# Turning keys and queries by VectorE in 32x32 blocks in a top-k attention and ELU feed-forward kernel

## The chip, the cores and the metric

The kernel runs on one core of a Trainium2 chip. The metric is the device time of one execution in microseconds. Three runs of the kernel before gave 1654.08, 1654.47 and 1656.92 us; the median is 1654.47 us.

A core has five engines with an instruction queue each, which is worked off in order: TensorE (PE, with a separate row PEld for weight loads), VectorE (DVE), ScalarE (ACT), GpSimd (POOL) and SyncE (SP), which here issues nearly all DMAs. Engines wait for each other through semaphores.

## The reference

```python
# q, k, v: (8, 8, 576, 64) float32; top_k = 32
scores = scale * np.matmul(q, k.transpose(0, 1, 3, 2))      # scale = 1/8
kth = np.partition(scores, -top_k, axis=-1)[..., -top_k:-top_k + 1]
scores = np.where(scores >= kth, scores, -1000000000.0)
scores = scores - np.max(scores, axis=-1, keepdims=True)
attn = np.exp(scores)
attn = attn / (np.sum(attn, axis=-1, keepdims=True) + 1e-09)
x = np.matmul(attn, v).transpose(0, 2, 1, 3).reshape(4608, 512)
h = x @ w_in                                                # (512, 2048)
g = np.where(h > 0.0, h, np.exp(np.minimum(h, 0.0)) - 1.0)
return g @ w_out                                            # (2048, 512)
```

The weights arrive as 64-bit floats and are converted to 32 bits on the chip.

## The kernel before

**Steps.** There are 8 batches of 8 heads. Heads go in pairs (`hp`, four a batch): partitions 0 to 63 hold the 64 dimensions of the first head of a pair, 64 to 127 those of the second. The 576 query rows of a batch are four tiles of 128 rows and one of 64. A step is one query tile with one head pair (for the tile of 64 rows, two pairs), 18 steps a batch and 144 in all. In even batches the tile of 64 rows comes last, in odd batches first.

**One step.** `scores` (L305) multiplies queries and keys on PE into two PSUM tiles, and ACT evicts them to `sc` with the scale (L313). VectorE then finds the 32nd largest value of each row: four times the eight largest (MAX8, lines 324, 334, 347, 359), with three passes in between that overwrite what was found (MATCH_REPLACE8, L328, L352). The first eight steps use `select_row`, where Tile's scheduler puts the instructions of each engine in order; later ones use `select`, in the order in which the program writes them (`manual_schedule` for PE, ACT, VectorE and POOL; SP's order is still the scheduler's). `mask` makes probabilities from the scores on ACT (L378, L381, L382) and POOL (L380), `normalise` divides them by their sums on POOL (L392 to L399), `turn` transposes them in 128x128 blocks on PE (L418, evicted by ACT at L419), `attend` multiplies them by v (L444), and `finish` puts the result into `xT` (L471).

**Feed-forward.** When the rows of a block are complete, its pieces join a list: `hidden` (L516 on PE; L526, L529, L531 on ACT), closing the ELU on VectorE (the gates, L488), and `project` (L541), with an output store (L550, L553). `feed` hands out pieces in every quarter of a step, by fixed costs and due times (L617 to L640); none of this depends on run time.

**In what order a step is written (from step 9 on).** Scores of the step two ahead, attention of a finished group, the first two passes of the top-k, pieces, mask of the step before, `turn_qk`, more passes, `turn` of the step two back, more passes and pieces, `normalise`, `turn_qk(True)`.

**Weights.** In the first ten steps `decode_piece` converts 32 pieces of the weights. A piece takes passes on POOL (L174, L191), three on ACT (L180, L181, L183) and one on VectorE (L187); eight raw buffers take the loads (L153).

**Keys and queries.** `load_qk` (L222) loads a head pair so that partition p holds the rows 4p to 4p+3 of both heads, 256 bytes for each row and head, and puts the last 64 rows of keys and queries into a fifth chunk of the key tile. Six DMAs go out for a pair. There are two buffers of each tile. `transpose_qk` (L255) is a generator: PE transposes the fifth chunk (L264), ACT copies it to two places (L267, L271); then for the keys, and after a `yield` for the queries, PE transposes four chunks (L275) and ACT copies them (L281). `turn_qk()` runs one part, `turn_qk(True)` the rest. So column c*128 + p of a head's queries is row 4p + c, and a query tile is every fourth row; `load_v` reads v in the same order (L247), and the output rows are written with a stride of four (L590). The first head's keys end in the last 64 rows, the second head's begin with them (L304), so that one chunk of the probabilities holds the rest of both heads.

`kqT` and `vT` have five buffers each. From batch 1 on, loads and turns are written at fixed steps before the first step `f` of the batch:

```python
plan = ((7, 5, 2), (5, 3, -2), (3, 1, -2), (1, -1, -3))
if b % 2 == 1:
    plan = ((7, 5, 0), (6, 4, -2), (5, 3, -3), (4, 2, -3))
for hp, (ahead, ready, late_v) in enumerate(plan):
    at(f - ahead, load_qk, b, hp)
    at(f - ready, start_qk, b, hp)
```

Of the kernel before, what the change touches and what calls it, by code (L numbers as in the profile page):

```python
# [10 lines left out]
FP32 = mybir.dt.float32  # L11
# [70 lines left out]
def kernel(  # L82
# [9 lines left out]
    nc = tc.nc  # L92
    P = nc.NUM_PARTITIONS
    B, H, S, D = q.shape
    dm, dff = moe_w_in.shape[0], moe_w_in.shape[1] // 2
    J = S // P
    JP = J * P
    R = S - JP
    HS = S // 2
# [2 lines left out]
    NF = dff // P  # L102
    NG = NF // 2
    T = 3 * P
    KEYS, QUERIES = R, R + S
    scale = 1.0 / float(D) ** 0.5
    assert D == 64 and R == 64 and J == 4 and H % 4 == 0 and dm == H * D == 512
    assert B % 2 == 0 and TOP_K % 8 == 0
# [1 line left out]
    def pool(name, bufs, **kw):  # L110
        return ctx.enter_context(tc.tile_pool(name=name, bufs=bufs, **kw))

    const = pool("const", 1)
    ldpool = pool("ld", 2)
    kvpool = pool("kv", 5)
# [7 lines left out]
    ps_t = pool("ps_t", 2, space=PSUM)  # L123
    ps_f = pool("ps_f", 2, space=PSUM)
    wide = [ps_sc.tile([P, 2, JP], FP32, tag=f"s{i}", name="scps") for i in range(2)]
# [6 lines left out]
    ident = const.tile([P, P], FP32, tag="ident", name="ident")  # L132
# [87 lines left out]
    loaded, kqT, vT = {}, {}, {}  # L220

    def load_qk(b, hp, other=nc.sync):  # L222

        for name, src in (("k", k), ("q", q)):
            n, queue = (J + 1, nc.sync) if name == "k" else (J, other)
            t = ldpool.tile([P, n, 2, D], FP32, tag=name + "in", name=name + "in")
            if name == "k":
                last = t
            for hh in range(2):
                queue.dma_start(  # L230
                    t[:, 0:J, hh, :],
                    src[b, 2 * hp + hh, 0:JP, :].rearrange("(p j) d -> p j d", j=J),
                )
            queue.dma_start(
                last[0:R, J, :, :] if name == "k" else last[R:P, J, :, :],
                src[b, 2 * hp : 2 * hp + 2, JP:S, :].rearrange("h p d -> p h d"),
            )
            loaded[b, hp, name] = t

    def load_v(b, hp):  # L240

        t = kvpool.tile([P, 2 * J + 2, D], FP32, tag="vT", name="vT")
        for hh in range(2):
            h = 2 * hp + hh
            nc.sync.dma_start(
                t[:, hh * J : (hh + 1) * J, :],
                v[b, h, 0:JP, :].rearrange("(p j) d -> p j d", j=J),  # L247
            )
            mine = slice(hh * R, (hh + 1) * R)
            other = slice((1 - hh) * R, (2 - hh) * R)  # L250
            nc.gpsimd.memset(t[other, 2 * J + hh, :], 0.0)
            nc.sync.dma_start(t[mine, 2 * J + hh, :], v[b, h, JP:S, :])
        vT[b, hp] = t

    def transpose_qk(b, hp):  # L255

        d = kvpool.tile([P, 4 * J + 3, D], FP32, tag="kqT", name="kqT")  # L260
        kqT[b, hp] = d[:].rearrange("p c d -> p (c d)")
        srcs = [loaded.pop((b, hp, name)) for name in ("k", "q")]
        ps = wide[0][:, 1, HS : HS + P]
        nc.tensor.transpose(  # L264
            ps, srcs[0][:, J, :, :].rearrange("p h d -> p (h d)"), ident[:]
        )
        nc.scalar.copy(  # L267
            d[:, 2 * J + 1 : 4 * J + 3 : 2 * J + 1, :],
            ps.rearrange("p (a s) -> p a s", a=2),
        )  # L270
        nc.scalar.copy(d[:, 0, :], ps[:, 0:R])  # L271
        for i, src in enumerate(srcs):
            ps = ps_t.tile([P, JP], FP32, tag="t", name="qkps")
            for c in range(J):
                nc.tensor.transpose(  # L275
                    ps[:, c * P : (c + 1) * P],
                    src[:, c, :, :].rearrange("p h d -> p (h d)"),
                    ident[:],
                )
            c0 = KEYS + i * (2 * J + 1) * D  # L280
            nc.scalar.copy(kqT[b, hp][:, c0 : c0 + JP], ps[:])  # L281
            yield

    def start_qk(b, hp):
        turning.append(transpose_qk(b, hp))
# [10 lines left out]
    def scores(u):  # L296

        u.sc = scpool.tile([P, 2, S], FP32, tag="sc", name="sc")
        q0 = QUERIES + u.t.qt * P
        for half in range(2):  # L300
            for h, i, rows in u.heads:
                kq = kqT[u.t.b, h // 2]
                part = slice(i * D, (i + 1) * D)
                k0 = (KEYS if i == 0 else 0) + half * HS  # L304
                nc.tensor.matmul(  # L305
                    wide[i][rows, half, 0:HS],
                    kq[part, q0 : q0 + u.t.ql],
                    kq[part, k0 : k0 + HS],
                    start=True,
                    stop=True,  # L310
                )
        for i in range(2):
            nc.scalar.activation(  # L313
                u.sc[:, i, :].rearrange("p (a s) -> p a s", a=2),
                wide[i][:, :, 0:HS], AF.Copy, scale=scale,
            )
# [253 lines left out]
    for b in range(B):  # L570
        if b % 2 == 0:
            rest = 2 * J
            division = [(0,), (1,), (2,), (3,), (rest,), (4, 5), (6, 7)]
            if b > 0:
                division = [(0, 1), (2, 3), (rest, 4, 5), (6, 7)]
            slots = {}
            for part in division:
                blk = Block(len(blocks), len(part))
                blocks.append(blk)
                slots.update((x, (blk, s)) for s, x in enumerate(part))  # L580
        first[b] = len(steps)
        tiles = []
        for qt in range(J + 1):
            r0 = b * S + (JP if qt == J else qt)
            if qt == J:
                (blk, slot), c0, n = slots[rest], (b % 2) * R, R
                rows = slice(r0, r0 + R)
            else:
                (blk, slot), c0, n = slots[(b % 2) * J + qt], 0, P
                rows = slice(r0, r0 + J * (P - 1) + 1, J)  # L590
            c0 += slot * P
            t = Tile(b, qt, rows, blk, slice(c0, c0 + n))
            blk.left += NHP
            blk.tiles[slot].append(t)
            tiles.append(t)
        order = [(0, 1), (2, 3), (J,)] if b % 2 == 0 else [(J,), (0, 1), (2, 3)]
        if b == 0:
            order[:2] = [(0,), (1,), (2,), (3,)]
        for qts in order:
            for hp in range(NHP // 2 if qts == (J,) else NHP):  # L600
                group = Group([tiles[qt] for qt in qts], hp)
                steps += [Step(tiles[qt], hp, group, i) for i, qt in enumerate(qts)]
            for qt in qts:
                n = len(steps)
                tiles[qt].block.ready = n + 1.0 if n <= tight else n + 2.5
# [11 lines left out]
    for b in range(1, B):  # L617
        f = first[b]
# [6 lines that stand above are left out]
            at(f - late_v, load_v, b, hp)  # L625
# [18 lines left out]
    E = mybir.EngineType  # L644
    engines = {E.PE, E.Activation, E.DVE, E.Pool}
    load_qk(0, 0, nc.scalar)
    load_weight(0)
    load_qk(0, 1)
    load_weight(1)
    load_v(0, 0)  # L650
    load_weight(2)
    with tc.manual_schedule(engines=engines):
        for hp in range(2):
            start_qk(0, hp)
            turn_qk(True)
            scores(steps[hp])
    load_qk(0, 2)
    load_qk(0, 3)
    for hp in range(1, NHP):
        load_v(0, hp)  # L660
# [8 lines left out]
    main, rest, other = slice(0, J), slice(J, J + 1), slice(J + 1, 2 * J + 1)  # L669
    for n in range(NS + 3):  # L670
# [3 lines left out]
        if n < tight:  # L674
            turn_qk(True)
            if n < 3:
                scores(ahead)
            if n > 1:
                scores(step(n + 3))
            for i in range(2):  # L680
                passes = select_row(cur, i, n < tight - 1)
                next(passes)
                if i == 0:
                    while closing:
                        attend(closing.pop(0))
                elif prev:
                    normalise(prev)
                    turn(prev, main)
                    turn(prev, rest)
                    turn(prev, other)  # L690
                feed(n, 0.25)
                next(passes)
                mask(cur, i, True)
                feed(n, 0.25)
            continue
# [64 lines left out]
```

## Time and profile before

| | |
|---|---|
| median of 3 runs | 1654.47 us |
| the profiled execution | span 1651.1 us from the first to the last instruction; the page gives no other time of it |
| mean granted TensorE clock | 0.976 |
| busy: PE, VectorE, ACT, POOL | 1592.8, 1496.6, 1152.7, 576.4 us |
| DMA queue q1 | 99792 packets, 54.26 MB, 11.8% of 16 engines |
| chain that ended last | PE 67%, VectorE 24%, ACT 4%, POOL 2% |

Busy time is the union of an engine's instructions. Instructions of an engine overlap at their ends: the time from one start to the next (the pitch) is shorter than the duration of one. A group's row gives line, engine, operation, tiles, shapes and count, then busy time and mean ns of one, then the idle time ahead and what ended it. A timeline row gives start and duration in us, then engine, line, operation and tiles; a count at the end means that several were merged.

### The profile page before, as it was taken

To read this page: it belongs to the slowest core of one execution; us is meant where nothing else is said; L and a number is where in the kernel's file an instruction comes from. 1 tells how busy PE (TensorE), PEld (TensorE's weight loads), DVE (VectorE), ACT (ScalarE), POOL (GpSimd) and SP (SyncE) were. 2 spreads that over 40 slices of the span, in tenths; PEclk is the share of its full clock that TensorE was granted. 3 is DMA by queue.
4 is the path that set the end of the run, shared out by engine and by line. 5 is a ranking of instruction groups with operands and counts; after the bars stand their busy time and mean duration, and the time that the engine had idled before them with its cause. 6 is when DMAs were issued, how large, how long until landed. Compare 5 with 4: busy or idle time off the path is not lost.

```text
span 1651.1 us, 25682 instructions
## 1 busy us (share of the span) xinstructions
PE 1592.8 (96%) x8528; PEld 1031.8 (62%) x8528; DVE 1496.6 (91%) x3044; ACT 1152.7 (70%) x2393; POOL 576.4 (35%) x1415
## 2 busy tenths in 40 slices
PE   5788999999999999999999999999999999999999
PEld 3476777666675757555566676656557575756564
DVE  6988999999999999999999999999989999998500
ACT  6898777678675867678576776768758585857521
POOL 4774333333333333333333333323323233332200
PEclk8579999999999999999999999999999999999999
DMA  7630110011100210011100210001200101000000
GB/s 227 188 116 8 44 38 20 7 29 44 35 1 14 52 43 8 7 29 44 29 13 1 56 30 28 1 21 36 50 13 1 36 8 29 7 7 7 7 13 13
DMA packets 101124, 56.19 MB, mean 34 GB/s; under 512 B 84096, under 2 KB 92288, under 8 KB 100992
## 3 DMA queue, kind: packets, MB, share of 16 engines
q1 hardware_dynamic: 99792, 54.26, 11.8%
q8 instruction: 68, 1.11, 0.3%
q14 instruction: 64, 0.52, 0.1%
q10 hardware_dynamic: 1200, 0.30, 0.1%
HBM read 45.09 MB, written 9.44 MB: 33 GB/s over the span
## 4 chain that ended last, share of the span: by engine, by line
PE 67%; DVE 24%; ACT 4%; POOL 2%; issue 1%; DMA 1%; SPq 0%; ACTq 0%; POOLq 0%; DVEq 0%
PE ops L541 24%; PE hps L516 22%; DVE wk L352 9%; DVE m L359 8%; PE avps L444 8%; PE scps L305 7%; PE eps L418 5%; DVE m L347 3%; DVE gT L488 1%; DVE wk L328 1%; PE qkps L275 1%; DVE m L334 1%; ACT sc L382 1%; PE scps L418 1%; ACT sc L381 1%
## 5 line engine op out<-in xcount | busy, mean ns | idle before, releaser
L359 DVE MAX8 m<-wk 128x8 f32<-128x576 f32 x816 | 574.7, 745 | 0.0
L516 PE MATMUL hps<-xT,w_in 128*128 128x256 f32 (+2 forms) x2432 | 546.1, 373 | 0.2 <-ACT xT L471 0.2
L541 PE MATMUL ops<-w_out,gT 128*128 128x512 f32 x1152 | 522.4, 598 | 0.0
L516 PEld LDWEIGHTS hps<-xT,w_in 128*128 128x128 f32 x2432 | 405.0, 192 | 97.5 <-issue 25.1
L352 DVE MATCH_REPLACE8 wk<-m,wk 128x576 f32<-128x576 f32 x544 | 399.3, 741 | 0.0
L541 PEld LDWEIGHTS ops<-w_out,gT 128*128 128x128 f32 x1152 | 208.5, 190 | 232.4 <-issue 219.5
L392 POOL TENSOR_SCALAR dene<-den 128x2 f32<-128x2 f32 x144 | 34.6, 240 | 818.9 <-ACT sc L382 818.5
L382 ACT ACTIVATE sc<-sc,den 128x576 f32<-128x576 f32 x288 | 223.5, 776 | 38.6 <-POOL den L380 14.5
L381 ACT ACTIVATE sc<-sc,m 128x576 f32<-128x576 f32 x288 | 227.0, 788 | 32.0 <-DVE m L359 31.9
L313 ACT ACTIVATE sc<-scps 128x576 f32<-128x576 f32 x288 | 173.3, 657 | 73.6 <-PE scps L305 73.4
L399 POOL TENSOR_SCALAR sc<-sc,rec 128x576 f32<-128x576 f32 x288 | 219.4, 772 | 15.0 <-POOL rec L397 0.2
L419 ACT COPY et<-eps 128x512 f32<-128x512 f32 x288 | 166.5, 578 | 80.1 <-PE eps L418 80.1
L305 PE MATMUL scps<-kqT 64*128 64x288 f32 (+1 forms) x1280 | 204.1, 443 | 18.3 <-ACT kqT L281 9.1
L444 PE MATMUL avps<-et,vT 128*64 128x256 f32 (+2 forms) x2080 | 194.7, 328 | 8.0 <-ACT et L419 7.5
L352 DVE MATCH_REPLACE8 wk<-m,sc 128x576 f32<-128x576 f32 x272 | 199.7, 741 | 0.0
L488 DVE SCALAR_TENSOR_TENSOR gT<-n,gT 128x512 f32<-128x512 f32 (+1 forms) x132 | 99.3, 752 | 107.6 <-ACT n L531 107.6
L418 PEld LDWEIGHTS eps<-ident,sc 128*128 128x128 f32 x1152 | 144.3, 144 | 82.0 <-issue 49.6
L347 DVE MAX8 m<-sc 128x8 f32<-128x576 f32 x272 | 191.1, 743 | 0.0
L418 PE MATMUL eps<-ident,sc 128*128 128x128 f32 x1152 | 176.5, 279 | 13.0 <-POOL sc L399 11.7
L444 PEld LDWEIGHTS avps<-et,vT 128*64 128x64 f32 x2080 | 123.1, 142 | 83.0 <-issue 25.1
L305 PEld LDWEIGHTS scps<-kqT 64*128 64x128 f32 (+1 forms) x1280 | 109.4, 183 | 89.0 <-issue 44.3
L526 ACT ACTIVATE n<-hps 128x512 f32<-128x512 f32 (+1 forms) x156 | 87.7, 562 | 83.1 <-PE hps L516 80.4
(49 smaller groups left out, 1089.1 us busy)
## 6 DMA issues: line engine op xcount, KB each, us to landing
kin<-in_k_dram SPq DMA_DIRECT2D x64, 128.0 KB, 2.9
raw<-in_moe_w_in_dram SPq DMA_DIRECT2D x16, 512.0 KB, 5.8
vT<-in_v_dram SPq DMA_DIRECT2D x64, 128.0 KB, 2.2
raw<-in_moe_w_out_dram SPq DMA_DIRECT2D x16, 512.0 KB, 3.4
out_dram<-osb SPq DMA_DIRECT2D x32, 256.0 KB, 2.3
qin<-in_q_dram SPq DMA_DIRECT2D x62, 128.0 KB, 2.8
kin<-in_k_dram SPq DMA_DIRECT2D x32, 32.0 KB, 2.5
vT<-in_v_dram SPq DMA_DIRECT2D x64, 16.0 KB, 2.1
```

The costliest lines, as they stand in the source:

```text
L305: nc.tensor.matmul(wide[i][rows, half, 0:HS], kq[part, q0 : q0 + u.t.ql], kq[part, k0 : k0 + HS], start=True, stop=True,)
L313: nc.scalar.activation(u.sc[:, i, :].rearrange("p (a s) -> p a s", a=2), wide[i][:, :, 0:HS], AF.Copy, scale=scale,)
L347: nc.vector.max(found[i], cur[i])
L352: nc.vector.match_replace(wk[i], found[i], cur[i], TAKEN)
L359: nc.vector.max(found[i], cur[i])
L381: nc.scalar.activation(sc, sc, AF.Prelu, scale=-1.0, bias=low, alpha=1.0 / STEEP)
L382: nc.scalar.activation(sc, sc, AF.Exp, scale=-STEEP, bias=gap, accum_out=u.den[:, i : i + 1])
L399: nc.gpsimd.tensor_scalar(u.sc[:, i, :], u.sc[:, i, :], rec[:, i : i + 1], 1.0, ALU.mult, ALU.mult)
L418: nc.tensor.transpose(ps[:, c * P : (c + 1) * P], sc[:, c0 : c0 + P], ident[:])
L444: nc.tensor.matmul(ps[i * D : (i + 1) * D, cols], vt[:, 2 * J + i if c == J else i * J + c, :], w, start=(c == 0), stop=(c == J),)
L516: nc.tensor.matmul(blk.h[:, f % bank, :], w_in[:, i, f * P : (f + 1) * P], blk.xT[:, i, 0:n_tok], start=(i == 0), stop=(i == NC - 1),)
L541: nc.tensor.matmul(blk.o[:], blk.gT[f // NG][:, f % NG, s * P : (s + 1) * P], w_out[:, f, :], start=(f == 0), stop=(f == NF - 1),)
```

## The change

Keys and queries are loaded as columns of half heads: partition 32*(2*hh + half) + i of the tile holds, for each of the 18 blocks n of 32 rows, the 32 dimensions of half `half` of row 32n + i of head `hh`. A piece is 32 floats, 128 bytes. One VectorE instruction for the keys of a pair and one for the queries then transposes every 32x32 block, which puts dimension d of head hh on partition 64*hh + d, with the rows in their natural order. The second head's last 64 keys are loaded into the first two blocks, so that the order of its keys is as before. A pair now takes ten DMAs, six for the keys and four for the queries. PE's nine transposes and ACT's four copies for a pair are gone. Since the rows are in natural order, v is read in rows of 256 bytes, and query tiles and output rows are contiguous. Loads and turns stay at the same places in the program.

```diff
-    KEYS, QUERIES = R, R + S
+    Q = 32
+    NB = S // Q
...
     def load_qk(b, hp, other=nc.sync):
-        for name, src in (("k", k), ("q", q)):
-            n, queue = (J + 1, nc.sync) if name == "k" else (J, other)
-            t = ldpool.tile([P, n, 2, D], FP32, tag=name + "in", name=name + "in")
-            if name == "k":
-                last = t
+        for name, src, queue in (("k", k, nc.sync), ("q", q, other)):
+            t = ldpool.tile([P, NB, Q], FP32, tag=name + "in", name=name + "in")
             for hh in range(2):
-                queue.dma_start(
-                    t[:, 0:J, hh, :],
-                    src[b, 2 * hp + hh, 0:JP, :].rearrange("(p j) d -> p j d", j=J),
-                )
-            queue.dma_start(
-                last[0:R, J, :, :] if name == "k" else last[R:P, J, :, :],
-                src[b, 2 * hp : 2 * hp + 2, JP:S, :].rearrange("h p d -> p h d"),
-            )
+                cut = NB if name == "q" or hh == 0 else NB - R // Q
+                for half in range(2):
+                    rows = slice((2 * hh + half) * Q, (2 * hh + half + 1) * Q)
+                    for lo, hi, to in ((0, cut, NB - cut), (cut, NB, 0)):
+                        if lo == hi:
+                            continue
+                        queue.dma_start(
+                            t[rows, to : to + hi - lo, :],
+                            src[
+                                b,
+                                2 * hp + hh,
+                                lo * Q : hi * Q,
+                                half * Q : (half + 1) * Q,
+                            ].rearrange("(n i) d -> i n d", i=Q),
+                        )
             loaded[b, hp, name] = t
...
     def load_v(b, hp):
-                v[b, h, 0:JP, :].rearrange("(p j) d -> p j d", j=J),
+                v[b, h, 0:JP, :].rearrange("(j p) d -> p j d", j=J),
...
     def transpose_qk(b, hp):
-        d = kvpool.tile([P, 4 * J + 3, D], FP32, tag="kqT", name="kqT")
-        kqT[b, hp] = d[:].rearrange("p c d -> p (c d)")
-        srcs = [loaded.pop((b, hp, name)) for name in ("k", "q")]
-        ps = wide[0][:, 1, HS : HS + P]
-        nc.tensor.transpose(
-            ps, srcs[0][:, J, :, :].rearrange("p h d -> p (h d)"), ident[:]
-        )
-        nc.scalar.copy(
-            d[:, 2 * J + 1 : 4 * J + 3 : 2 * J + 1, :],
-            ps.rearrange("p (a s) -> p a s", a=2),
-        )
-        nc.scalar.copy(d[:, 0, :], ps[:, 0:R])
-        for i, src in enumerate(srcs):
-            ps = ps_t.tile([P, JP], FP32, tag="t", name="qkps")
-            for c in range(J):
-                nc.tensor.transpose(
-                    ps[:, c * P : (c + 1) * P],
-                    src[:, c, :, :].rearrange("p h d -> p (h d)"),
-                    ident[:],
-                )
-            c0 = KEYS + i * (2 * J + 1) * D
-            nc.scalar.copy(kqT[b, hp][:, c0 : c0 + JP], ps[:])
+        d = kvpool.tile([P, 2, S], FP32, tag="kqT", name="kqT")
+        kqT[b, hp] = d
+        for i, name in enumerate(("k", "q")):
+            src = loaded.pop((b, hp, name))
+            nc.vector.transpose(d[:, i, :], src[:].rearrange("p n d -> p (n d)"))
             yield
...
     def scores(u):
-        q0 = QUERIES + u.t.qt * P
+        q0 = u.t.qt * P
-                k0 = (KEYS if i == 0 else 0) + half * HS
+                k0 = half * HS
-                    kq[part, q0 : q0 + u.t.ql],
-                    kq[part, k0 : k0 + HS],
+                    kq[part, 1, q0 : q0 + u.t.ql],
+                    kq[part, 0, k0 : k0 + HS],
...
-            r0 = b * S + (JP if qt == J else qt)
+            r0 = b * S + qt * P
-                rows = slice(r0, r0 + J * (P - 1) + 1, J)
+                rows = slice(r0, r0 + P)
```

## The prediction

> **What bounds the kernel now.** I read the page's first two parts first, for which engine is nearly full and when. The rows of part 2 are 40 slices of 41 us.
>
> ```profile
> PE 1592.8 (96%) x8528; PEld 1031.8 (62%) x8528; DVE 1496.6 (91%) x3044; ACT 1152.7 (70%) x2393; POOL 576.4 (35%) x1415
> ...
> PE   5788999999999999999999999999999999999999
> ...
> DVE  6988999999999999999999999999989999998500
> ```
>
> Both PE and DVE stand at 9 nearly throughout, so the averages decide nothing. The table by stretches does; its columns are us, then busy PE, PEld, DVE, ACT, POOL, granted clock, DMA share, GB/s.
>
> ```profile
> 0.00:164.00 164.00, 124.47 (x648) 89.14 (x649) 135.80 (x277) 134.82 (x275) 97.08 (x155) 0.78 0.44 135
> 164.00:700.00 536.00, 525.33 (x3234) 358.47 (x3234) 536.00 (x1100) 392.75 (x821) 190.11 (x502) 0.99 0.10 26
> 700.00:1552.00 852.00, 848.09 (x4325) 528.88 (x4322) 818.67 (x1661) 600.06 (x1250) 282.88 (x742) 1.00 0.08 22
> 1552.00:1651.00 99.00, 94.88 (x328) 55.27 (x326) 6.17 (x9) 25.04 (x49) 6.32 (x16) 1.00 0.04 14
> ```
>
> There are four stages. From 164 to 700 VectorE has no idle time at all: every added VectorE microsecond is paid. From 700 to 1552 PE is the fuller one (3.9 us idle) and VectorE idles 33.3 us. After 1552 the top-k is over and PE works off the feed-forward remainder. Before 164 neither is full, and I read the chain and the timeline there. The VectorE timeline puts the idle time of the third stage in front of the gates, as the list of waits does:
>
> ```profile
> DVE gT L488 <- ACT n L531: 107.6, 29, 44.5
> ```
>
> About 64 of the 107.6 us lie in the tail; 20.6 lie between 850 and 1341, and 12.8 after 1341.
>
> **The change, part by part.** *PE work removed.* Each of the 32 (batch, head pair) turns loses nine 128x128 transposes.
>
> ```profile
> 917.76 0.60 PE L275 MATMUL qkps<-ident,kin 128*128 128x128 f32 x4
> 918.19 0.60 PE L418 MATMUL eps<-ident,sc 128*128 128x128 f32 x4
> ```
>
> Four take 0.60 us but the next group starts 0.43 later, so the pitch is 0.11: 9 x 0.11 = 1.0 us a turn, 32 us in all, not the 50.7 us of the groups' summed durations (20.7 + 20.4 + 9.6). *ACT work removed:* two copies of 0.59, one of 0.25 and one of 0.21 a turn: 1.6 us, 53 in all. In the middle ACT is 70-73% busy, so this hides behind VectorE or PE; it counts only in the start.
>
> *VectorE work added.* 64 transposes of 128x576. No such operation is in the trace. The rows nearest in shape are these, with their pitch from the chain of waits:
>
> ```profile
> L359 DVE MAX8 m<-wk 128x8 f32<-128x576 f32 x816 | 574.7, 745 | 0.0
> ...
> 17.06 1.46 DVE wk L328 x2
> 18.52 1.32 DVE m L334 x2
> ```
>
> That is 0.66 us a MAX8 pass, 0.73 a match-replace pass. Lower end: the 128x512 shift of L187 mostly took 0.41, scaled 576/512 = 0.46. Upper end: two passes of 0.73 = 1.46, if a 4-byte block turn needs two. I take 0.67, the one-pass rows of the same width. The Trainium skill's page "VectorE: DVE Perf Modes", section "The three transpose paths", gives 311 ns for 128 columns of bf16 on VectorE and 390 ns on TensorE; scaled by 4.5 columns that would be an estimate of 1.40 us each and 47 us more in the sum. The trace's TensorE transposes come every 0.11 us, far below the page's figure, so I read that table as single latencies.
>
> *The steady part.* 56 transposes (batches 1 to 7) fall after 164. Those of batches 1 to 3 come before 700: 24 x 0.67 = +16 us, paid in full. The other 32 come before 1341 (the last batch turns at steps 121 to 124): +21.4, against the 20.6 us of VectorE waits on PE in that stretch. PE loses 16 us there and VectorE slows, so I expect most of that wait to go: -18. After 1341 nothing is turned, PE stays the limit, and only the lead that PE brings there counts: the eviction of a step's scores ends 20 to 25 us before the first top-k pass on them from 300 to 760, and 12 to 20 us before it later, so some 6 us of lead can come back; I take -4 (0 to -8). Together: 16 + 21.4 - 18 - 4 = +15. If no wait goes, +37; if every wait before 1341 goes and 8 in the tail, +9.
>
> *Waits that move.* The transposes sit in VectorE's queue in the midst of a step (keys) and at its end (queries). Queued behind them is the top-k itself, and who waits for that is ACT's mask. They wait for a load and for a free kqT buffer (five). In odd batches pair 1's buffer is freed by the scores issued at the start of the same step, 1.2 us of PE; PE leads or trails VectorE by about 3 us, so 0 to 3 us in four places, which I take as 0 since PE gains slack. Loads: in odd batches pairs 2 and 3 landed 14 to 19 us before use; four more DMA issues of 0.63 us take 2.5 of that. Other SP work (v, out) is queued behind, with longer margins. Cost 0; a missing load would stop the top-k for up to 10 us.
>
> *DMA volume.* 73,728 pieces of 256 B become 147,456 of 128 B, and v goes from 8,192 of 1 KB to 32,768 of 256 B. The packet records show 17.9 ns mean for 256 B and 9.0 for 4 B; between these, q and k need 83 to 165 us of each of 16 engines where they needed 82. The share in the middle is 0.08 to 0.10, and stays under 0.2: no cost. The page "DMA: Bandwidth & Descriptors" speaks against the change, in "Why small descriptors are slow (HBM only)": fixed cycles a packet, 11 for 256 B; the same formula makes 7 for 128 B, an estimate of 1.3 times the engine time, inside my bounds.
>
> *The start.* This is where order matters. Before, PE turns and ACT copies ran ahead, and the top-k of step 1 followed that of step 0 at once:
>
> ```profile
> 15.65 1.42 DVE L324 MAX8 m<-sc 128x8 f32<-128x576 f32 x2 [0.73 <-ACT sc L313]
> ...
> 20.85 1.19 ACT L313 ACTIVATE sc<-scps 128x576 f32<-128x576 f32 x2 [0.38 <-PE scps L305]
> ```
>
> Step 3 began at 45.6. In the changed kernel as built, VectorE's queue has pair 1's query transpose behind the last pass of step 0, pair 2's at the end of step 1, pair 3's at the end of step 2; each is directly ahead of the step whose scores need it. ACT's queue has the masks of step n ahead of the scores' eviction of step n+1, and PE's has the probability transposes of step 1 ahead of the scores of step 2. I follow it by hand. Keys land near 7, turned by 8.4; the first weight's conversion (loaded 1.2 us later) holds ACT until 12.0, so step 0 starts at 12.7 (3.0 earlier). A step is 9.63 us plus a key transpose: last pass at 23.0, query turned at 23.7. ACT masks until 25.8 (0.14 + 0.66 + 0.76 twice), converts a weight, evicts: step 1 at 28.9, 5.2 idle. Step 1 with a wait on a weight ends at 40.1, query at 40.8. Then masks (41.7), POOL's normalising (29.45 to 32.89 in the old timeline: 3.4), PE's eight transposes, scores, eviction: step 2 at 48.4, 7.6 idle. Step 2 ends at 58.7; masks and eviction give step 3 at 62.3, 2.9 idle. Against 45.6: +16.7.
>
> ACT tells the same from its side: until step 3 it idles 36 us of 62, where it idled 13 of 45.6. After that decode binds on ACT (gaps of 1 to 3 us only between 46 and 165), so 23 more idle minus 6 us of copies removed is +17. I take +16; bounds +3 (the later stalls before 164, 13.1 us on VectorE, all give way) and +27 (decode pieces that ran early now crowd steps 3 to 8: four more at 2 us, with three more waits).
>
> **Sum.** 1651.1 + 16 + 15 = 1682. The median run is 3.4 above the span of the profiled execution; with that, 1685.5.
>
> **Rivals.** (1) *PE decides to the end.* The chain that ended last is 67% PE. If the last 950 us are PE's alone and the start costs nothing, the gain is the removed PE pitch from 700 on, 16 us, plus 12 before it: 1654.5 - 28 = 1626 at best, 1638 with the later part only. Against it: VectorE's 536.00 of 536.00. It decides only if a transpose costs under 0.3 us and the start's stalls are absent. Chance 0.05. (2) *The gains cancel:* start +3, steady +9 less a cheap transpose (56 x 0.21 = 12): about 1654 to 1660. Chance 0.05, of which 0.02 within 0.2%, what a measurement of this kernel can tell from no change. (3) *The transpose is two passes:* 56 x 0.79 = 44 more, +3 in the start: 1733. For it: 4-byte elements, nothing in the trace. Chance 0.08. (4) *VectorE stands before late loads or buffers,* 28 turns by 1 to 3 us: 1713 to 1770. Against it: margins of 14 us. Chance 0.04. That the turn is not moved is excluded: the built queue has 64 transposes on VectorE and none of q or k on PE.
>
> **How the numbers follow.** The forecast, slower with one pass of VectorE a turn, has 0.78. Its range is from +3 and +9 (1666) to +27 and about +27 (1708). That leaves out rivals 1 and 2 and most of 3 and 4, some 2 in 10 with the forecast's own ends, so the range is 1664 to 1710. Faster 0.05, same 0.02, slower 0.93.
>
> **What would show it.** VectorE busy up by 43 us to about 1540, transposes near 0.74 duration. Three VectorE gaps of 3 to 8 us before 62 us, released by ACT's eviction of scores, and step 3 at about 62. No VectorE gap from 180 to 850, and few gate waits between 870 and 1380. PE's idle time up by more than 32 us. Wrong if the transpose is off 0.67 by a third, if step 3 starts before 50, or if gate waits remain over 10 us before step 125.

## The result, and the profile after

The changed kernel takes 1700.55 us (median of 4 runs, 1698.03 to 1703.54) against 1654.28 us for the kernel before, measured along with it. The ratio is 1.028, with a 95% interval of 1.0263 to 1.0296. The change makes the kernel slower by 46 us; the forecast was 1685.5 in a range of 1664 to 1710.

The first parts of the page of the changed kernel show where to look. As before, the rows of part 2 are 40 equal slices, here of 42.5 us.

```profile
PE 1583.7 (93%) x8240; PEld 1009.5 (59%) x8240; DVE 1539.2 (90%) x3108; ACT 1112.2 (65%) x2265; POOL 577.1 (34%) x1415
...
PE   2668979999999979999999989999999989999999
...
DVE  5697899999999999999999999999999999998600
```

VectorE is busy 42.6 us more, PE only 9.1 us less. VectorE's row now reads 9 from the sixth slice to the 36th, shortly before the top-k ends, and PE's row has 7s and 8s in it. The new group of instructions is this one:

```profile
L266 DVE STREAM_TRANSPOSE kqT<-kin 128x576 f32<-128x576 f32 x32 | 24.4, 762 | 7.0 <-DMA kin<-in_k_dram 7.0
L266 DVE STREAM_TRANSPOSE kqT<-qin 128x576 f32<-128x576 f32 x32 | 24.4, 761 | 0.0
```

A transpose is a single pass: 0.76 us each, as MAX8 on the same width (0.745). In the timeline the next instruction starts 0.68 to 0.69 us after it. Only the very first waits for its load (7.0 us).

Steps make better marks than fixed times. Step 12 begins at 164.9 us before and at 194.2 after; step 63 at 685.1 and 734.4; step 125, the first behind the last turn, at 1341.4 and 1393.2; the last top-k pass ends at 1552.6 and 1603.5. The table by stretches between these marks, first of the kernel before, then of the changed one (us, busy PE, PEld, VectorE, ACT, POOL, clock, DMA share, GB/s):

```profile
0.00:164.90 164.90, 125.37 (x656) 90.04 (x657) 136.70 (x279) 135.72 (x278) 97.08 (x155) 0.78 0.44 135
164.90:685.10 520.20, 510.89 (x3169) 350.62 (x3167) 520.20 (x1068) 381.95 (x797) 186.29 (x491) 0.99 0.10 27
685.10:1341.40 656.30, 651.03 (x3301) 405.01 (x3300) 635.73 (x1293) 466.22 (x977) 220.09 (x574) 1.00 0.10 25
1341.40:1552.60 211.20, 211.20 (x1086) 131.18 (x1084) 198.44 (x401) 144.23 (x298) 66.60 (x179) 1.00 0.03 10
```

```profile
0.00:194.20 194.20, 122.61 (x620) 85.17 (x621) 143.83 (x287) 131.68 (x262) 97.65 (x155) 0.97 0.43 114
194.20:734.40 540.20, 511.59 (x3047) 343.86 (x3046) 535.97 (x1091) 365.40 (x749) 186.81 (x491) 0.97 0.13 26
734.40:1393.20 658.80, 645.08 (x3186) 395.83 (x3184) 655.59 (x1325) 450.48 (x920) 223.97 (x583) 0.99 0.12 25
1393.20:1603.50 210.30, 210.12 (x1067) 129.69 (x1068) 198.21 (x401) 140.07 (x288) 62.40 (x170) 0.99 0.04 10
```

The first number behind each stretch is its length. The start is 29.3 us longer, the second stretch 20.0, the third 2.5, and the fourth 0.9 shorter; the rest loses 0.4. Together 50.5 us between the two profiled executions (spans 1651.1 and 1701.6). The profiled execution of the changed kernel was the slowest of its four runs, 1703.54 us in its own time, so the parts add up to 4 us more than the medians do.

In the start, the VectorE timeline of the changed kernel has three new waits, each ahead of the first pass of a step:

```profile
28.01 1.42 DVE L309 MAX8 m<-sc 128x8 f32<-128x576 f32 x2 [0.73 <-ACT sc L298]
...
50.40 1.42 DVE L309 MAX8 m<-sc 128x8 f32<-128x576 f32 x2 [9.96 <-ACT sc L298]
...
64.60 1.42 DVE L309 MAX8 m<-sc 128x8 f32<-128x576 f32 x2 [3.12 <-ACT sc L298]
```

Step 1 shows only 0.73 here because a weight pass (L188) stands between; it had waited 3.49 us just before. Step 3 begins at 64.6, where it began at 45.6.

### The profile page after: what moved, and what is told of

Its sections match the earlier page's. It is cut to its first block, busy times and chain, and to the rows that moved or that the text cites. A ratio compares the mean times of both kernels' runs of the same rounds, so it can differ in the third digit from the quotient of the medians.

```text
span 1701.6 us, 25296 instructions
## 1 busy us (share of the span) xinstructions
PE 1583.7 (93%) x8240; PEld 1009.5 (59%) x8240; DVE 1539.2 (90%) x3108; ACT 1112.2 (65%) x2265; POOL 577.1 (34%) x1415
## 4 chain that ended last, share of the span: by engine, by line
PE 57%; DVE 33%; ACT 5%; issue 2%; POOL 1%; DMA 1%; SPq 1%; DVEq 0%; ACTq 0%; POOLq 0%
PE ops L526 22%; PE hps L501 17%; DVE wk L337 13%; DVE m L344 10%; PE avps L429 7%; PE scps L290 6%; PE eps L403 4%; DVE m L332 4%; DVE gT L473 2%; DVE kqT L266 2%; ACT sc L367 1%; ACT et L404 1%; DVE wk L313 1%; ACT sc L366 1%; DVE m L319 1%
## 5 line engine op out<-in xcount | busy, mean ns | idle before, releaser
L290 PE MATMUL scps<-kqT 64*128 64x288 f32 (+1 forms) x1280 | 212.2, 457 | 72.4 <-DVE kqT L266 63.9
L298 ACT ACTIVATE sc<-scps 128x576 f32<-128x576 f32 x288 | 172.8, 655 | 108.7 <-PE scps L290 108.6
L429 PE MATMUL avps<-et,vT 128*64 128x256 f32 (+2 forms) x2080 | 204.9, 332 | 11.0 <-ACT et L404 10.7
L429 PEld LDWEIGHTS avps<-et,vT 128*64 128x64 f32 x2080 | 128.2, 144 | 90.8 <-issue 33.3
```

Source lines behind the costliest of these rows:

```text
L290: nc.tensor.matmul(wide[i][rows, half, 0:HS], kq[part, 1, q0 : q0 + u.t.ql], kq[part, 0, k0 : k0 + HS], start=True, stop=True,)
L429: nc.tensor.matmul(ps[i * D : (i + 1) * D, cols], vt[:, 2 * J + i if c == J else i * J + c, :], w, start=(c == 0), stop=(c == J),)
```

## The experiments

All are compared with the kernel before, which was measured along with them: 1654.7 us (12 runs) for experiments 1 to 4 and 1655.4 us (15 runs) for 5 to 8.

**1. Batch 0 by PE.** In `load_qk`, `load_v`, `transpose_qk`, `scores` and the output rows, batch 0 takes the path of the kernel before; its last 64 rows are loaded into a part of the kqT tile that is still free, since the key tile has no room for them. For example:

```diff
-                v[b, h, 0:JP, :].rearrange("(j p) d -> p j d", j=J),
+                v[b, h, 0:JP, :].rearrange(
+                    "(j p) d -> p j d" if b > 0 else "(p j) d -> p j d", j=J
+                ),
...
-                rows = slice(r0, r0 + P)
+                rows = slice(r0, r0 + P) if b > 0 else slice(r0, r0 + J * (P - 1) + 1, J)
```

> Batch 0 is loaded, turned and written as before the change, batches 1 to 7 as after it. Theory A (the loss is two separate terms: some 29 us in the first 12 steps, because VectorE's turns of batch 0 stand in its queue directly ahead of the steps that need them and decode lags, and some 22 us of VectorE passes paid later): the first term goes, 1654.3 + 22 = 1676, range 1671 to 1682, with step 3 near 46 and step 12 near 165. Theory B (loads in 128-byte pieces or late keys slow the kernel throughout): the loss of the later batches stays larger than the VectorE passes explain, 1685 or more. Theory C (PE's relief is worth something once the start is repaired): 1665 or less.

Measured: 1673.16 us, ratio 1.0113 (1.0098 to 1.0128). Step 3 began at 45.7 and step 12 at 165.1, as before the change. The second and third stretch:

```profile
165.10:703.10 538.00, 509.45 (x3047) 344.75 (x3046) 535.81 (x1091) 365.26 (x749) 186.68 (x491) 0.97 0.13 26
703.10:1360.90 657.80, 644.73 (x3186) 396.01 (x3184) 654.93 (x1326) 450.35 (x920) 223.05 (x583) 0.99 0.12 25
```

The start accounts for 27 of the 46 us. What is left, 18.4 us, is the second stretch (+17.8) and hardly the third (+1.5). Theory A holds, with 3 us less than it said.

**2. Batch 0's queries issued from ACT's queue.**

```diff
-    load_qk(0, 1)
+    load_qk(0, 1, nc.scalar)
...
-    load_qk(0, 2)
-    load_qk(0, 3)
+    load_qk(0, 2, nc.scalar)
+    load_qk(0, 3, nc.scalar)
```

> The changed kernel, with the queries of batch 0's pairs 1 to 3 issued from ACT's queue instead of SP's, so that they are issued earlier; as built, VectorE's queue then has pair 1's and half of pair 2's turns within step 0, and pair 3's before step 2 starts, instead of directly ahead of the steps that need them. Theory A (the start is lost by the place of the turns in VectorE's queue, not by their 5 us of work): step 3 starts near 50 instead of 64.6, and 10 to 25 of the 46 us come back: 1676 to 1691. Rival (the start is lost by loading and turning as such, or by decode whatever the order): step 12 stays near 194 and the time within 5 us of 1700.

Measured: 1680.28 us, ratio 1.0158 (1.0142 to 1.0173): 20 us of the 46 come back with the same turns on the same engine. Step 3 began at 48.4, step 12 at 172.8. In the VectorE timeline pair 1 is turned within step 0, and step 1 starts with no wait that the row shows:

```profile
14.53 0.78 DVE L266 STREAM_TRANSPOSE kqT<-kin 128x576 f32<-128x576 f32 x1 [1.30 <-DMA qin<-in_q_dram]
15.23 0.73 DVE L266 STREAM_TRANSPOSE kqT<-qin 128x576 f32<-128x576 f32 x1
...
26.00 1.40 DVE L309 MAX8 m<-sc 128x8 f32<-128x576 f32 x2
```

So most of the start's loss is the place of the turns in the queues, not their work. Earlier weights are not what brought it back: SP issues the second, third and fourth of them at 12.06, 15.38 and 33.20 us here, against 11.10, 13.90 and 33.92 in the changed kernel. Earlier issue of the queries and the new order of all queues came together in this run; it doesn't say which of ACT's and VectorE's orders did more.

**3. Every later turn done twice.**

```diff
-            nc.vector.transpose(d[:, i, :], src[:].rearrange("p n d -> p (n d)"))
+            for _ in range(2 if b > 0 else 1):
+                nc.vector.transpose(d[:, i, :], src[:].rearrange("p n d -> p (n d)"))
```

> The changed kernel, in which each of the 56 VectorE transposes of batches 1 to 7 is done twice into the same place; nothing else changes. Theory A (VectorE is the limit from step 12 to about step 125): 56 x 0.68 = 38 us less the few microseconds of gate waits left there (about 9): 1700.6 + 29 to 38 = 1730 to 1739. Rival (PE is the limit in the later half, and a VectorE pass is half hidden there): about 56 x 0.68 x 0.5 = 19, 1715 to 1722.

Measured: 1743.91 us, 43 us above the changed kernel, more than the 38 that I allowed and above theory A's range. The rows of two transposes show why: two into the same place take 1.58 us, and the next instruction starts 1.50 after the first, so the second costs 0.8, not 0.68.

```profile
200.84 1.58 DVE L267 STREAM_TRANSPOSE kqT<-kin 128x576 f32<-128x576 f32 x2
202.34 0.06 DVE L338 MATCH_VALUE_LOAD wk<-m,sc 128x8 f32 x1
```

56 x 0.8 = 45. The second and third stretch:

```profile
189.30:747.00 557.70, 514.68 (x3047) 345.31 (x3045) 554.87 (x1115) 365.41 (x749) 187.87 (x491) 0.96 0.12 25
747.00:1430.50 683.50, 652.72 (x3186) 398.10 (x3184) 679.54 (x1357) 450.24 (x920) 224.85 (x583) 0.98 0.12 24
```

They grew by 17.5 and 24.7 us over the changed kernel, 0.73 and 0.77 for each added pass: with the first pass in place VectorE is the limit in both, and another pass is paid almost fully everywhere. The rival, half hidden, is out.

**4. The changed kernel without later turns.** Batches 1 to 7 take over the turned tiles of batch 0.

```diff
     def transpose_qk(b, hp):
+        if b > 0:
+            kqT[b, hp] = kqT[0, hp]
+            for name in ("k", "q"):
+                loaded.pop((b, hp, name))
+                yield
+            return
```

> The changed kernel without any turn of batches 1 to 7: they are loaded, but scores use the turned keys and queries of batch 0. Neither PE nor VectorE turns anything after the start. Theory A (VectorE pays its passes up to 700, and PE is the limit afterwards as before the change): the start's 29 us stay, the passes of batches 1 to 3 come back, and after 700 PE's missing transposes give 16 us less than before: 1654.3 + 29 - 16 = 1667, range 1660 to 1675. Rival (PE's missing transposes count from the start on, 28 us): 1655 or less. Second rival (128-byte loads cost time by themselves): 1680 or more.

Measured: 1659.17 us, ratio 1.0025 (1.0015 to 1.0034); 0.8 below my range. The second and third stretch:

```profile
190.40:710.00 519.60, 510.20 (x3062) 342.01 (x3060) 519.60 (x1067) 366.23 (x749) 187.65 (x491) 0.99 0.21 39
710.00:1348.60 638.60, 637.03 (x3166) 390.91 (x3166) 634.32 (x1293) 447.15 (x915) 220.32 (x574) 1.00 0.05 13
```

The parts are as theory A has them. The second stretch lasts 519.6 us, against 520.2 before the change, although PE has no turn in it; the third lasts 638.6 against 656.3. Of the miss of 8 us, 3.5 are the start, which took 190.4 us here (+25.5, not +29); the rest lies in the later stretches, which together gave 20.3 us where 16 had been expected.

**5. The kernel before with loads in 128-byte pieces.**

```diff
-                queue.dma_start(
-                    t[:, 0:J, hh, :],
-                    src[b, 2 * hp + hh, 0:JP, :].rearrange("(p j) d -> p j d", j=J),
-                )
+                for cols in (slice(0, 32), slice(32, 64)):
+                    queue.dma_start(
+                        t[:, 0:J, hh, cols],
+                        src[b, 2 * hp + hh, 0:JP, cols].rearrange("(p j) d -> p j d", j=J),
+                    )
...
```

> The kernel before, in which every load of keys and queries is cut into two half-row columns: pieces of 128 bytes instead of 256, twelve DMAs a pair instead of six; PE turns them as before. Theory A (the small pieces cost nothing off the start, and the start is lost by order): 1654.7 to 1662, with step 3 within 3 us of 45.6. Theory B (small pieces cost time by themselves): 1665 to 1690.

Measured: 1663.88 us, ratio 1.0049 (1.0036 to 1.0063). Both theories missed by a little: it lies between them, and step 3 began 4.0 us later. But it is all in the start. Step 12 began at 175.5, 10.6 us late, and after that the stretches are those of the kernel before:

```profile
175.50:695.50 520.00, 511.01 (x3169) 350.64 (x3167) 520.00 (x1067) 381.53 (x798) 185.02 (x491) 0.99 0.13 27
695.50:1352.90 657.40, 652.74 (x3301) 405.66 (x3300) 636.14 (x1294) 466.17 (x977) 218.13 (x574) 1.00 0.12 25
```

Off the start twice as many pieces cost next to nothing (-0.2 and +1.1 us). In the start they (here with six more issues a pair, in the changed kernel four) push the weights back on SP's queue: the fourth is issued at 27.85 us in the kernel before, at 41.78 here and at 33.92 in the changed kernel. So a part of the changed kernel's 29 us, perhaps up to these 10.6, can be the loads themselves; the split between loads and order was not measured more finely.

**6. The kernel before without later turns.** The same edit as in experiment 4, made in the kernel before.

> The kernel before without any turn of batches 1 to 7: they are loaded, but scores use the turned keys and queries of batch 0. This is what PE's transposes and ACT's copies cost where they stood. Theory A (PE is the limit only from 700 on): about 18 us less, 1637, range 1632 to 1642; from step 12 to step 63 nothing. Rival (PE's chain decides through the whole run): 28 us or more, 1627 or less.

Measured: 1636.78 us, ratio 0.9888 (0.9874 to 0.9901): 18.6 us less. Again the second stretch doesn't move (520.1 us), and the third takes 639.4 instead of 656.3:

```profile
166.90:687.00 520.10, 510.02 (x3062) 342.09 (x3060) 520.10 (x1067) 365.96 (x750) 187.12 (x491) 0.99 0.10 26
687.00:1326.40 639.40, 638.18 (x3166) 391.70 (x3166) 634.37 (x1294) 446.68 (x915) 217.86 (x574) 1.00 0.04 13
```

VectorE's gate waits in the third fall from 20.6 us to this row:

```profile
DVE gT L494 <- ACT n L537: 5.0, 5, 1.6
```

This is all that PE's and ACT's turning costs after the start, and so the most that moving it elsewhere could bring.

**7. Only the late queries by VectorE.** The first 512 query rows of batches 4 to 7 are loaded as half heads and turned by VectorE, and the output rows of these batches become contiguous; keys, and the rest of the queries, stay with PE.

```diff
+    def by_vector(b):
+        return b > 3
...
         for i, src in enumerate(srcs):
+            if i == 1 and by_vector(b):
+                c0 = KEYS + (2 * J + 1) * D
+                nc.vector.transpose(kqT[b, hp][:, c0 : c0 + JP], src)
+                yield
+                continue
```

> The kernel before, in which only the first 512 query rows of batches 4 to 7 are loaded in half-head columns and turned by VectorE (16 transposes of 128x512), the rest by PE as before. Theory A (in that stretch PE is the limit and VectorE waits 20 us; half of the turns moved balances the two): PE loses about half of the 18 us, VectorE gains 16 x 0.61 = 10 us of its 20 idle: 1654.7 - 8 = 1647, range 1643 to 1652. Rival (a VectorE pass costs its time wherever it stands): 1655 to 1665.

Measured: 1647.81 us, ratio 0.9953 (0.9939 to 0.9967): 7.6 us faster than the kernel before and 53 faster than the changed one. VectorE gains 16 passes of 0.70 us and loses most of its gate waits in the third stretch (20.6 us before the change), which now takes 651.3 us, 5.0 less:

```profile
687.50:1338.80 651.30, 646.40 (x3247) 399.09 (x3246) 644.28 (x1309) 459.57 (x963) 216.75 (x574) 1.00 0.11 26
...
DVE gT L508 <- ACT n L551: 7.0, 6, 2.1
```

**8. The same from batch 1 on.**

```diff
-        return b > 3
+        return b > 0
```

> As the run before, with batches 1 to 7 instead of 4 to 7: 12 more transposes of 128x512 lie where VectorE has no idle time. Theory A: 12 x 0.61 = 7 us more than that run, about 1654, range 1650 to 1660. Rival (PE's relief counts there too): no more than 2 us above that run.

Measured: 1658.39 us, ratio 1.0019 (1.001 to 1.0028): 10.6 us above experiment 7. The second stretch accounts for 6.8 of it (526.9 us between its steps 12 and 63, against 520.1), which is twelve passes at 0.57; the start and the third stretch are 1.2 and 1.3 us longer. The same operation gains in one half of the run and costs in the other.

## Why the prediction was right, point by point

The measured time lies in the range, 15 us above the forecast. The sum had 16 + 15 = 31 us; between the profiled executions it came out as 50.5, 13.3 more in the start and 6.2 more after it. Both errors go the same way, so nothing cancelled by luck; the range held because the start's bounds had made it wide.

**The limit by stage.** Shown. Between steps 12 and 63 VectorE alone sets the time: taking PE's turns away altogether gave 0.1 us there before the change and leaves 519.6 after it (experiments 6 and 4). From 63 to 125 it was PE before the change: the same removal gave 17 us, against the 16 of the prediction. In the changed kernel VectorE's passes have used up its waits there, and it is the limit in that stretch too (experiment 3). Rival 1, PE deciding to the end, is refuted by this, not by the total alone.

**The price of a transpose.** Right: 0.68 in the queue, against the 0.67 taken from MAX8. The bounds of 0.46 and 1.46 were wide. The estimate of 1.40 from the Trainium skill's table ("VectorE: DVE Perf Modes", The three transpose paths) is refuted by the 0.76 of the row. Rival 3, two passes, falls with it.

**The second stretch.** +16 predicted, +20.0 measured. VectorE's busy time grew by 15.8, as worked out; 4.2 are two gate waits at 257 and 683, which the prediction did not have. In experiment 1 they are 2.2.

**The third stretch.** +21.4 of passes less 18 of waits, +3.4 in all, predicted; +2.5 measured. VectorE's waits for gates went from 20.6 to 3.2:

```profile
DVE gT L473 <- ACT n L516: 3.2, 2, 2.9
```

**The lead brought to the tail.** Mis-sized: -4 predicted, -1.3 measured. In the changed kernel the eviction of scores leads VectorE by 24 to 26 us from step 124 to 126, but by 18.7 at step 127 and less afterwards, and the tail runs as before.

**The start.** This is the term that was off: +16 taken, +29.3 in the profiled execution, 25.5 and 24.4 in those of experiments 4 and 3, whose starts are the same. The hand count up to step 3 held: 62.3 predicted against 64.6, with waits of 5.2, 7.6 and 2.9 us against 4.2, 10.0 and 3.1. Of the 2.4 us that the second wait was longer, one can be PE's pace: the scores of the step took 2.29 us there, and 1.24 at PE's full pace (last section). What failed is the step from there on, "I take +16": the loss was 19.0 us at step 3 and grew by 10.3 up to step 12. ACT had idled 40.7 of 64.6 us, and three weight pieces were converted where the kernel before had seven. VectorE then waits 21.4 us for weights and gates between steps 3 and 12, where it waited 13.1 (the second and third row are from 82 us on):

```profile
75.31 0.43 DVE L188 TENSOR_SCALAR raw<-raw 128x512 uint32<-128x512 uint32 x1 [3.75 <-ACT raw L182]
...
DVE gT L473 <- ACT n L516: 16.4, 4, 6.1
DVE raw L188 <- ACT raw L182: 1.2, 1, 1.2
```

The bounds had such a case as +27, with four pieces more and three more waits, and the measured 24 to 29 us lie about there. That the four late pieces make these waits is read from the rows, not tested. Between these two steps ACT was busy 4.0 us more than before the change (107.8 against 103.8) and PE 6.2 us more (106.1 against 99.9); PE ran at its slow pace there up to at least 117 us. How much each of them did stays open.

**DMA volume and late loads.** Right off the start: no transpose after the first waits for a load or a buffer, so rival 4 falls. Experiment 4 keeps all loads of the changed kernel, those of v in 256 bytes among them, and its second stretch is no longer than before the change. At 12.7 ns a piece q and k took 117 us of each DMA engine, 1.4 times as much as before and inside the bounds of 83 to 165; the prediction's estimate was 1.3 times. Experiment 5 shows that the price in the start is not nothing: there it was 10.6 us.

**The signs.** VectorE's busy time, the length of a transpose, step 3 near 62 us and PE's idle time (58.3 us before, 117.9 after) came as written, and so did the three waits, but for the 10.0 us of the second, which was to be 8 at most. Two went against it. "No VectorE gap from 180 to 850" meets three waits for gates, 6.1 us ahead of 187, 2.2 ahead of 259 and 2.0 ahead of 685. And gate waits before step 125 come to 23.9 us, where over 10 was to be a sign of being wrong: 16.4 of them lie in the start, the term that was mis-sized, and 7.4 behind step 12.

## What to carry to other kernels

A step moved from one engine to another is worth what the stage allows: here the turns cost 20 us where VectorE was the limit and 2.5 where it had waited for PE anyway, and there half as many, of queries alone, gained 7.6 us. Read which engine has no idle time stage by stage, and move only as much work as fills the other's idle time. In a start that a scheduler orders, look where the moved instruction lands in every queue: a short one directly ahead of the step that needs it brings the whole latency chain with it, and what idles meanwhile may have to be caught up later.

## What the runs showed of the hardware that was not expected

The granted clock of the profile does not tell the pace of matmuls ahead of its first record. From 41 to 82 us it reads 0.58 in the kernel before and 1.00 in the changed one, where PE is busy less:

```profile
41.00:82.00 41.00, 29.91 (x124) 20.25 (x123) 39.88 (x82) 36.37 (x74) 31.09 (x46) 0.58 0.62 192
```

```profile
41.00:82.00 41.00, 24.40 (x85) 14.42 (x86) 24.54 (x50) 18.30 (x37) 13.79 (x26) 1.00 0.22 82
```

Yet the eight score matmuls took 2.29 us in the changed kernel at 47.40 and again at 61.63, and 1.24 us at 23.54 in the kernel before:

```profile
23.54 1.24 PE L305 MATMUL scps<-kqT 64*128 64x288 f32 x8 [0.85 <-ACT kqT L271]
```

```profile
47.40 2.29 PE L290 MATMUL scps<-kqT 64*128 64x288 f32 x8
```

The clock records kept in the two traces begin at 22.3 us in the kernel before and at 126.8 us in the changed one, and the column counts the time ahead of the first record as full speed. Behind it the durations follow the records: in the kernel before they read 1.0 at 23.54, where the eight took 1.24 us, and 0.5 from 29.1 to 70.1 us, where they took 2.29 (at 30.49). Ahead of the first record they took 2.29 us in both kernels. In the changed one every score matmul up to 117 us had the slow pace, and the first with the fast one started at 128.72. So the 1.00 is at fault here, and the 0.97 in the first row of the changed kernel's table by stretches is too high. The Trainium skill ("TensorE: Matmul & The Clock Gate", Part 1: The HAM clock gate) says that the array runs at half rate after an idle window and at full rate after some 3.4 us of steady work. The two durations (a ratio of 1.85) agree with two such rates; how long a pause or a stretch of work must be was not tested here.

A 128-byte piece took 12.7 ns on average in the packet records of the changed kernel, a 256-byte piece 17.9 before: half the bytes for 0.71 of the time.
